# Last stage of a spectral mix and a decayed sum: channel-major result with gated last matrices, eight frequency units for nine, even places by accumulating transfers

## The chip, the cores and the metric

The kernel runs on one core of one Trainium2 chip. The core has a matrix engine (TensorE, PE in the profile, with PEld for its weight loads), a vector engine (DVE), a scalar engine (ACT), GpSimd (POOL), a queue engine that mostly issues transfers (SP), and 16 DMA engines. The engines share two memories: SBUF (128 partitions) and PSUM, which TensorE writes and DVE and ACT read. The metric is the device time of one execution in microseconds (us); lower is better.

## The reference

The input x has 2048 places and 512 channels. A gate g, one number for each place, mixes two results. The first is a filter in the frequency plane: a real two-dimensional Fourier transform, a product with complex weights, and the inverse. The second is a long convolution along the places with a kernel made from the channel's parameters, plus a skip term.

```python
g = sigmoid((x * gate_w).sum(-1, keepdims=True))
X = rfft2(x) * (w_r + 1j * w_i)
a = irfft2(X, s=(2048, 512))
dt = exp(log_dt)
A = -exp(log_A_real) + 1j * A_imag
C = (C_real + 1j * C_imag) * dt[:, None]
K = 2 * Re(einsum("dn,dnl->dl", C, exp(A * dt * pos)))
b = causal_conv(x, K) + x * D_skip
return g * a + (1 - g) * b
```

The arithmetic is float32. The kernel computes, per channel, whether `A * dt` is so small over 2048 places that K is a constant. If it is for all 512 channels (it is for these inputs), the convolution is a running sum of x times a number per channel, and the long general branch behind `tc.If` is not entered.

## The kernel before

**Order.** No scheduler is at work: `PLAN` is a list of words, a letter for a function and a number for its piece, and the program issues them in that order. Each engine works through its own words in that order. A tile of a pool (`ps` with 4 PSUM buffers, `blk` with `NBLK`, `w`, `v`, `short`) is reused once its last reader is done, so a word may also wait for a buffer.

**First stage** (`C`, `c`). x is loaded in pieces (`PARTS`). `C` runs small matrices over 64 partitions for each piece, for some pieces on sums and differences that POOL forms first (`F`); `c` turns the result on DVE (`STREAM_TRANSPOSE`) into `AR`. Every later unit reads all of `AR`.

**Middle stage, nine units.** The frequencies along the places are held in slots, two to a unit; unit 8 (`pr == 8`) is half as large and holds slot 0's and slot 16's leftovers. For each unit: `P` (TensorE, second transform), `t` (ACT copy to SBUF), `D` (TensorE, transform along channels), `d` (ACT copy), `Z` (four DVE instructions), `U` and `W` (DVE products with the weights), `p` and `g` (two POOL instructions each), `h` (ACT, one row), `I` (TensorE, transform back along channels), `i` (ACT copy) and `V` (two DVE instructions into `AI`). The weights of a unit are loaded by SP (`l`), and one row of them is overwritten (`L`).

**The running sum**, beside it, four quarters k of the channels. `x` and `y` (ACT) scale the even and the odd places; `m` is a DVE scan that gives the sums at the odd places; `n` (POOL) forms the even places by a subtraction; `o` (ACT) scales x by the skip factor; `r` (POOL queue) adds the sums to `XT` by a transfer of 1 MB that accumulates. `G` is the gate: TensorE, ACT, and a transfer that lays g with places on partitions (`g1`).

**Last stage.** `K` fixes slot 0, `B` (TensorE) and `b` (DVE transposes) give `VA`. The second result is brought from channels to places on partitions by TensorE transposes (`Y`), times 1 - g on the way out of PSUM (`s`, ACT). `Q` (TensorE) is the last matrix, eight blocks j of four matrices with 256 columns; `q` (DVE) or `a` and `A` (ACT, POOL) multiply by g and add, and SP stores.

Of the kernel before, what the change touches and what calls it, by code (L numbers as in the profile page):

```python
# [9 lines left out]
F32 = mybir.dt.float32  # L10
# [5 lines left out]
P = 128  # L16
# [4 lines left out]
NWARM = 10  # L21
NV = 2
# [16 lines left out]
PARTS = [slice(a, b) for a, b in zip([0, 4, 8, 16, 24, 32, 40, 48, 56], [4, 8, 16, 24, 32, 40, 48, 56, 64])]  # L39
# [3 lines left out]
def _consts():  # L43
# [37 lines left out]
    s2e = s2[:17][..., K2].reshape(17, 128, 128).transpose(1, 0, 2)  # L81
# [10 lines left out]
    s2p[2, 0, :, :, 1], s2p[2, 1, :, :, 1] = np.cos(th), -np.sin(th)  # L92

# [12 lines left out]
    s2r = np.stack([v.reshape(2, 32, 2, 128).transpose(2, 1, 0, 3).reshape(128, 128) @ inv for v in s2p[1:]], 1)  # L106
# [12 lines left out]
    s1b = s1b.reshape(32, 128, 64).transpose(1, 0, 2)  # L119
# [3 lines left out]
    for x in range(2):  # L123
# [29 lines left out]
        "c_s2v": f32(s2v), "c_s2r": f32(s2r), "c_s2q": f32(s2q), "c_s1b": f32(s1b), "c_s1a": f32(s1a.reshape(128, 4, 8, 128).transpose(1, 0, 2, 3)), "c_dfw": f32(dfw), "c_dbw": f32(dbw),  # L153
# [5 lines left out]
def body(ctx: ExitStack, tc: tile.TileContext, x, xg, xt, w, wh, prms, vecs, gw, dskip,  # L159
# [21 lines left out]
    AI = work.tile([P, 17, D], F32, name="AI")  # L181
# [28 lines left out]
    with tc.manual_schedule():  # L210
        prm = [blk([P, 4, P], "prm") for _ in range(3)]
        ldt = few[:, 0]
        nc.scalar.dma_start(s1e, c_s1e)
# [578 lines left out]
```

## Time and profile before

| | |
|---|---|
| time before, median of 3 runs | 131.91 us (130.80 to 132.53) |
| the profiled execution, its own time | 130.77 us |
| its span in the profile | 128.8 us |
| mean granted TensorE clock | 0.954 |
| ACT busy, share of the span | 61.9 us, 48% |
| DMA moved | 26.56 MB, mean 206 GB/s |

The span is shorter than the execution's own time by 1.97 us. In the rows of the timeline the first number is the start in us from the span's start, the second the time, `xN` the number of instructions in the row, and the bracket the idle time ahead of it with what ended it. Float32 matrices are recorded as two instructions each, so x16 is eight matrices.

### The profile page before, as it was taken

How to read it: one execution, taken by the hardware profiler on the slowest of the kernel's cores; microseconds unless marked ns; L12 is line 12 of the kernel's file. 1: busy time of each engine (PE TensorE's matmuls, PEld its weight loads, DVE VectorE, ACT ScalarE, POOL GpSimd, SP SyncE). 2: the span in 40 equal slices, each digit the busy share in tenths (PEclk: the TensorE clock that was granted, in tenths of full speed). 3: DMA queues.
4: the chain of work that ended last, by engine and by line, in shares of the span. 5: the costliest groups of instructions: out<-in, count | busy, mean ns of one | idle time of the engine just before them, and what ended most of it. 6: DMA issues, size and time to landing. Idle time of an engine off the chain costs nothing. (4 is left out here: it accounts for less than half of the span.)

```text
span 128.8 us, 2226 instructions
## 1 busy us (share of the span) xinstructions
PE 105.1 (82%) x817; PEld 84.5 (66%) x817; DVE 90.8 (70%) x136; ACT 61.9 (48%) x111; POOL 70.4 (55%) x62
## 2 busy tenths in 40 slices
PE   6988977699699999909949999398999999999000
PEld 6954646585189979809939599287844788898000
DVE  0077896897998889999975999982369935526500
ACT  0021007955339769997538354444760295464000
POOL 0467120427399999999959799993000000786000
PEclk9999999999999999996899999869999999999975
DMA  3999999999476299998288697250000003355960
GB/s 109 414 356 409 428 396 384 400 394 354 176 267 232 80 251 243 279 239 258 88 163 163 122 198 233 100 163 5 0 0 5 0 0 140 130 221 204 377 257 7
DMA packets 9300, 26.56 MB, mean 206 GB/s; under 512 B 1696, under 2 KB 2496, under 8 KB 8256
## 3 DMA queue, kind: packets, MB, share of 16 engines
q1 hardware_dynamic: 8560, 22.07, 46.0%
q0 software_dynamic: 576, 4.19, 16.9%
q8 instruction: 8, 0.13, 0.4%
q14 instruction: 12, 0.10, 0.2%
q10 hardware_dynamic: 144, 0.07, 0.2%
HBM read 17.90 MB, written 4.19 MB: 171 GB/s over the span
## 5 line engine op out<-in xcount | busy, mean ns | idle before, releaser
L376 PE MATMUL p_t<-s2e,AR 128*128 128x128 f32 x136 | 19.0, 299 | 3.1 <-DMA s2e<-in_c_s2e_dram 2.2
L376 PEld LDWEIGHTS p_t<-s2e,AR 128*128 128x128 f32 x136 | 18.1, 211 | 5.1 <-ACT gs L328 1.9
L458 PE MATMUL p_v<-dbw,gt 128*128 128x128 f32 x136 | 16.8, 278 | 4.2 <-DVE v L308 3.2
L458 PEld LDWEIGHTS p_v<-dbw,gt 128*128 128x128 f32 x136 | 15.9, 192 | 5.4 <-DVE v L308 3.4
L392 PE MATMUL p_d<-et,dfw 128*128 128x256 f32 (+1 forms) x72 | 16.6, 375 | 1.9 <-DVE v L308 1.7
L540 POOL TENSOR_TENSOR AI<-AI,qs 128x1024 f32<-128x1024 f32 x2 | 4.8, 2383 | 21.7 <-ACT qs L536 21.7
L263 DVE STREAM_TRANSPOSE AR<-p_s 128x512 f32<-128x512 f32 (+1 forms) x18 | 10.4, 629 | 7.6 <-PE p_s L255 6.9
L392 PEld LDWEIGHTS p_d<-et,dfw 128*128 128x128 f32 x72 | 12.6, 190 | 4.4 <-ACT XT L315 1.8
L312 POOL TENSOR_TENSOR v<-v,uo 128x1024 f32<-128x1024 f32 x4 | 10.1, 2536 | 8.7 <-DVE v L308 8.7
L525 PE MATMUL p_oa<-AR,s1a 128*128 128x256 f32 x64 | 14.3, 379 | 0.0
L471 DVE TENSOR_TENSOR AI<-p_v,po 128x512 f32<-128x512 f32 (+1 forms) x18 | 10.8, 649 | 5.0 <-ACT po L463 5.0
L427 POOL TENSOR_TENSOR px<-tw 128x512 f32<-128x512 f32 (+1 forms) x9 | 12.2, 1354 | 3.8 <-DVE tw L420 3.7
L525 PEld LDWEIGHTS p_oa<-AR,s1a 128*128 128x128 f32 x64 | 11.8, 187 | 1.9 <-DVE AR L493 0.2
L439 POOL TENSOR_TENSOR gt<-px 128x512 f32<-128x512 f32 (+1 forms) x9 | 12.5, 1384 | 0.3
L440 POOL TENSOR_TENSOR gt<-px 128x512 f32<-128x512 f32 (+1 forms) x9 | 12.4, 1381 | 0.0
L428 POOL TENSOR_TENSOR px<-tw 128x512 f32<-128x512 f32 (+1 forms) x9 | 12.2, 1353 | 0.0
L255 PE MATMUL p_s<-AI 64*64 64x256 f32 (+1 forms) x192 | 10.7, 363 | 1.8 <-issue 0.7
L501 PE MATMUL p_y<-eye,XT 128*128 128x128 f32 x64 | 10.0, 314 | 2.2 <-issue 2.2
L501 PEld LDWEIGHTS p_y<-eye,XT 128*128 128x128 f32 x64 | 9.2, 200 | 3.4 <-issue 2.3
L381 ACT COPY et<-p_t 128x1024 f32<-128x1024 f32 (+1 forms) x9 | 8.7, 961 | 5.2 <-PE p_t L376 5.2
L255 PEld LDWEIGHTS p_s<-AI 64*64 64x64 f32 x192 | 7.2, 132 | 5.6 <-PE p_s L250 2.4
L418 DVE TENSOR_TENSOR tw<-p_d,w 128x1024 f32<-128x1024 f32 x8 | 9.7, 1217 | 0.6 <-DVE p_d L405 0.5
(67 smaller groups left out, 165.9 us busy)
## 6 DMA issues: line engine op xcount, KB each, us to landing
XT<-in_xt_dram SPq DMA_DIRECT2D x4, 1024.0 KB
w<-in_w_dram SPq DMA_DIRECT2D x8, 512.0 KB, 5.2
XT<-v POOLq DMA_DIRECT2D x4, 1024.0 KB, 9.5
AI<-in_x_dram SPq DMA_DIRECT2D x7, 512.0 KB, 6.3
s1a<-in_c_s1a_dram SPq DMA_DIRECT2D x4, 512.0 KB, 4.0
out_dram<-bs SPq DMA_DIRECT2D x8, 256.0 KB, 2.3
out_dram<-AI SPq DMA_DIRECT2D x8, 256.0 KB, 3.6
prm<-in_prms_dram SPq DMA_DIRECT2D x3, 256.0 KB, 5.9
```

What stands on the lines that cost most here:

```text
L255: T.matmul(p[64 * g:64 * g + 64, h, u * n:u * n + n], s1e[r, 64 * u * i:64 * u * i + 64], xin(q)[r, i, g * n:g * n + n], start=i == 0, sto ...
L263: V.transpose(av[:, u, :, k], pv[:, u])
L376: T.matmul(p[:, q, :, 64 * v:64 * v + 64], AR[:, q % 2, 8 * (q // 2) + sl // 2, :, sl % 2], s2e[:, k], start=True, stop=True)
L392: T.matmul(parts(u)[:, o, 1:3] if h else parts(u)[:, o, 0:4:3], dfw[:, 2 * h + o], t_["et", u][:, 2 * h + o, :, :n], start=True, stop=True)
L427: G.tensor_tensor(po[:, 0], t1[:, :, 0:4:2], t1[:, :, 1:4:2][:, :, ::-1], op=ALU.subtract)
L428: G.tensor_tensor(po[:, 1, :, ::-1], t2[:, :, 0:4:2], t2[:, :, 1:4:2][:, :, ::-1], op=ALU.add)
L439: G.tensor_tensor(gv[:, :, 0], src[0], src[1], op=ALU.subtract)
L440: G.tensor_tensor(gv[:, ::-1, 1], src[0], src[1], op=ALU.add)
L458: T.matmul(p[:, v, h, o], rows(u, o, v, h), dbw[:, h, o], start=True, stop=True)
L471: V.tensor_tensor(ai[:, :, :, k], t_["pi", u][:, :n, :, 0], t_["po", u][:, :n], op=ALU.subtract if k else ALU.add)
L501: T.transpose(p[:, k, i], xv[:, i, :, 4 * j + k], eye)
L525: T.matmul(p[:, k], s1a[j // 2][:, 4 * j % 8 + k], VA[:, :, 4 * j + k], start=True, stop=True)
```

## The change

Four things are changed together, and the order is written anew.

1. **Eight units.** Slot 16's part is packed into the empty half of slot 0, so unit 8 is gone and every unit is full. Column 0 of unit 0 now needs a few tiny instructions of its own in `Z` and `h`; `K` has one matrix for two.
2. **Even places by a transfer.** The scan writes only the odd places' sums, into half the tile. `n` is now an accumulating transfer of 512 KB of `-x * scale` into the even half of `XT`, and `r` adds the sums to both halves from a source that is read twice. The places of `XT` are stored as two halves, even and odd.
3. **Channel-major result.** The last matrix takes `VA` as the stationary side and the constant `s1a` as the moving side, so the result has channels on partitions: eight blocks of eight matrices with 128 columns for eight blocks of four with 256. `Y`, `s` and the transposes of the second result are gone. g goes to DRAM and back as four broadcast tiles `gb` (`G2`, `O`). `E` (DVE) multiplies `s1a` by g, read from a copy in PSUM that `u` (ACT) makes; `H` (POOL) multiplies `XT` by 1 - g, 128 x 1024 at a time; `q` (DVE) is one addition for each block.
4. **First stage.** Ten pieces, nothing loaded between them, and POOL forms only the sum for eight of them (`FOLDS`), not the difference.

The general branch behind `tc.If` is adapted to the new layout; it is still not entered for these inputs.

```diff
-NWARM = 10
-NV = 2
+NWARM = 7
+NV = 4
-UNITS = [8, 0, 1, 2, 3, 4, 5, 6, 7]
+FOLDS = [0, 0, 1, 1, 1, 1, 1, 1, 1, 1]
-            E.tensor_tensor(f[:, 1, :n], xv[:, 0], xv[:, 1], op=ALU.subtract)
+            if FOLDS[q] == 2:
+                E.tensor_tensor(f[:, 1, :n], xv[:, 0], xv[:, 1], op=ALU.subtract)
...
-            v = t_["v", k] = work.tile([P, L], F32, tag="v", name="v", bufs=NV)
-            V.tensor_tensor_scan(v[:, 1:L:2], t_["v1", k], t_["uo", k], 0.0, op0=ALU.add, op1=ALU.add)
-
-        def even(k, E):
-            v = t_["v", k]
-            E.tensor_tensor(v[:, 0:L:2], v[:, 1:L:2], t_["uo", k], op=ALU.subtract)
+            t_["v", k] = work.tile([P, 1024], F32, tag="v", name="v", bufs=NV)
+            V.tensor_tensor_scan(t_["v", k], t_["ve", k], t_["vo", k], 0.0, op0=ALU.add, op1=ALU.subtract)
+
+        def even(k):
+            G.dma_start(part(2 * k), t_["vo", k], accum_op=ALU.add)
...
-            G.dma_start(XT[:, k], t_["v", k], accum_op=ALU.add)
+            G.dma_start(XT[:, k].rearrange("p (z n) -> p z n", z=2), t_["v", k].rearrange("p (o n) -> p o n", o=1).broadcast_to([P, 2, 1024]), accum_op=ALU.add)
+
+        def load_g(k):
+            t_["gb", k] = work.tile([P, 1024], F32, tag="v", name="gb", bufs=NV)
+            nc.sync.dma_start(t_["gb", k], gd[k // 2][1024 * (k % 2):1024 * (k % 2) + 1024].rearrange("(o n) -> o n", o=1).broadcast_to([P, 1024]))
+
+        def near(k):
+            t_["gp", k] = psum("p_g").rearrange("p u n -> p (u n)")
+            S.copy(t_["gp", k], t_["gb", 2 + k])
+
+        def damp(h, E):
+            r = part(h)
+            E.tensor_tensor(r, r, t_["gb", h % 2], op=ALU.mult)
...
+        def gated(k, E):
+            s = s1a[k].rearrange("p b (e c) -> p b e c", e=2)
+            g = (t_["gp", k // 2] if E is V else t_["gb", 2 + k // 2]).rearrange("p (b c) -> p b c", c=64)[:, 8 * (k % 2):8 * (k % 2) + 8]
+            for e in range(2):
+                E.tensor_tensor(s[:, :, e], s[:, :, e], g, op=ALU.mult)
+
         def Q_(j):
-            p = t_["pq", j] = psum("p_oa").rearrange("p k (b d) -> p (k b) d", b=2)
-            for k in range(4):
-                T.matmul(p[:, k], s1a[j // 2][:, 4 * j % 8 + k], VA[:, :, 4 * j + k], start=True, stop=True)
+            i, k = j // 4, j % 4
+            p = t_["pq", j] = psum("p_oa").rearrange("p u (b c) -> p (u b) c", b=4)
+            for b in range(8):
+                T.matmul(p[:, b], VA[:, i, 8 * (k % 2) + b, :, k // 2], s1a[k][:, b], start=True, stop=True)
+
+        def last_a(j, E, p):
+            i, k = j // 4, j % 4
+            o = AF_[:, 1024 * j:1024 * j + 1024]
+            z, b = k // 2, 8 * (k % 2)
+            xv = XT[:, 2 * i:2 * i + 2].rearrange("p e (z c b) -> p e z c b", z=2, b=16)[:, :, z, :, b:b + 8]
+            E.tensor_tensor(o.rearrange("p (e c b) -> p e c b", e=2, b=8), p.rearrange("p b (e c) -> p e c b", e=2), xv, op=ALU.add)
+            nc.sync.dma_start(out[j], o)
...
-        def q_a(j):
-            for k in range(4):
-                b = 4 * j + k
-                V.scalar_tensor_tensor(BS(j)[:, k], t_["pq", j][:, k], g1[:, 0, b:b + 1], BS(j)[:, k], op0=ALU.mult, op1=ALU.add)
-            store(j)
...
```

The order of SP from the last pieces of x on, before. `AI` is where x lands, `s2e` and `dfw` are the matrices of `P` and `D`, `w` is a unit's weights; the parameters `prm` stand ahead of these rows, among the pieces of x.

```order
L216 DMA AI_68<-in_x_dram 128x1024 x2
L296 DMA XT_69<-in_xt_dram 128x2048
L550 DMA s2e_71<-in_c_s2e_dram 128x256
L550 DMA s2e_71<-in_c_s2e_dram 128x128
L296 DMA XT_69<-in_xt_dram 128x2048
L556 DMA s2e_71<-in_c_s2e_dram 128x1024
L553 DMA eye_61<-in_c_eye_dram 128x128
L557 DMA gws_77<-in_gate_w_dram 128x128
L557 DMA pers_70<-in_vecs_dram 128x4
L552 DMA AI_68<-in_wh_dram 128x72
L551 DMA dfw_74<-in_c_dfw_dram 128x512
L362 DMA w_251<-in_w_dram 128x1024
```

And now:

```order
L229 DMA AI_71<-in_x_dram 128x512 x2
L282 DMA prm_109<-in_prms_dram 128x512
L282 DMA prm_111<-in_prms_dram 128x512
L554 DMA s2e_75<-in_c_s2e_dram 128x768
L279 DMA last_73<-in_vecs_dram 128x4
L282 DMA prm_257<-in_prms_dram 128x512
L555 DMA s2e_75<-in_c_s2e_dram 128x1024
L552 DMA eye_61<-in_c_eye_dram 128x128
L551 DMA last_73<-in_wh_dram 128x64
L392 DMA w_307<-in_w_dram 128x1024
L392 DMA w_316<-in_w_dram 128x1024
L550 DMA dfw_78<-in_c_dfw_dram 128x512
```

All of x goes ahead of the parameters, and the matrices of `P` and `D` and the first two units' weights go ahead of the 1 MB pieces of `XT`.

The end of POOL's order, before. `px` and `gt` are the results of `p` and `g` of the last two units, `qs` is a block scaled by ACT.

```order
L439 TENSOR_TENSOR gt_752<-px_729 128x2x4x64
L440 TENSOR_TENSOR gt_752<-px_729 128x2x4x64
L427 TENSOR_TENSOR px_765<-tw_761 128x2x2x128
L428 TENSOR_TENSOR px_765<-tw_757 128x2x2x128
L439 TENSOR_TENSOR gt_768<-px_765 128x2x4x64
L440 TENSOR_TENSOR gt_768<-px_765 128x2x4x64
L540 TENSOR_TENSOR AI_68<-AI_68,qs_968 128x1024
L540 TENSOR_TENSOR bs_826<-bs_826,qs_994 128x1024
L540 TENSOR_TENSOR AI_68<-AI_68,qs_1016 128x1024
```

And now, with the semaphores that a row waits for (`DMASW` those of POOL's own transfers, numbered in turn; `DMASW6` is that of the row `XT_72<-vo_710`). `vo` and `v` are the sources of `n` and `r`, `gb` holds 1 - g.

```order
L459 TENSOR_TENSOR gt_796<-px_788 128x2x4x64
L331 DMA XT_72<-vo_710 128x1024 [waits DMAHW0_49,Activation_49]
L349 TENSOR_TENSOR XT_72<-XT_72,gb_782 128x1024 [waits DMAHW7_49,DMASW4_49]
L349 TENSOR_TENSOR XT_72<-XT_72,gb_786 128x1024 [waits DMAHW0_49,DMASW5_49]
L337 DMA XT_72<-v_763 128x2x1024 [waits DMASW6_49,DVE_49,Activation_49]
L349 TENSOR_TENSOR XT_72<-XT_72,gb_782 128x1024
L349 TENSOR_TENSOR XT_72<-XT_72,gb_786 128x1024
L349 TENSOR_TENSOR XT_72<-XT_72,gb_782 128x1024 [waits DMASW2_49]
L349 TENSOR_TENSOR XT_72<-XT_72,gb_782 128x1024 [waits DMASW7_49]
L349 TENSOR_TENSOR XT_72<-XT_72,gb_786 128x1024 x2
```

Behind the last unit POOL had three additions of blocks; it has the last `n`, two products with 1 - g, the last `r` (which waits for that `n`) and six more products.

The end of DVE's order, before. `p_v` is a unit's last PSUM tile, `p_ia` and `p_oa` are the tiles of `B` and `Q`.

```order
L471 TENSOR_TENSOR AI_68<-p_v_802,po_811 128x2x2x128 x2
L471 TENSOR_TENSOR AI_68<-p_v_831,po_849 128x2x2x128 x2
L493 STREAM_TRANSPOSE AR_64<-p_ia_859 128x16x2x32
L493 STREAM_TRANSPOSE AR_64<-p_ia_865 128x16x2x32
L493 STREAM_TRANSPOSE AR_64<-p_ia_871 128x16x2x32
L493 STREAM_TRANSPOSE AR_64<-p_ia_881 128x16x2x32
L493 STREAM_TRANSPOSE AR_64<-p_ia_889 128x16x2x32
L493 STREAM_TRANSPOSE AR_64<-p_ia_894 128x16x2x32
L493 STREAM_TRANSPOSE AR_64<-p_ia_899 128x16x2x32
L493 STREAM_TRANSPOSE AR_64<-p_ia_906 128x16x2x32
L546 SCALAR_TENSOR_TENSOR bs_826<-p_oa_952,g1_62,bs_826 128x256 x4
L546 SCALAR_TENSOR_TENSOR AI_68<-p_oa_973,g1_62,AI_68 128x256 x4
```

And now, in two pieces: the last `V` with what stands among them (`s1a<-s1a,p_g` is `E`), and the last transposes.

```order
L528 TENSOR_TENSOR s1a_692<-s1a_692,p_g_694 128x8x64 x2
L528 TENSOR_TENSOR s1a_675<-s1a_675,p_g_694 128x8x64 x2
L328 SCALAR_TENSOR_TENSOR v_763<-p_x_744,vo_710 128x1024
L493 TENSOR_TENSOR AI_71<-p_v_724,po_746 128x2x2x128 x2
L493 TENSOR_TENSOR AI_71<-p_v_754,po_770 128x2x2x128 x2
L493 TENSOR_TENSOR AI_71<-p_v_772,po_799 128x2x2x128 x2
L373 CAST count_62<-p_count_791 1x1
L528 TENSOR_TENSOR s1a_702<-s1a_702,p_g_815 128x8x64 x2
L493 TENSOR_TENSOR AI_71<-p_v_806,po_819 128x2x2x128 x2
L528 TENSOR_TENSOR s1a_748<-s1a_748,p_g_815 128x8x64 x2
```

```order
L515 STREAM_TRANSPOSE AR_67<-p_ia_865 128x32x16x2
L515 STREAM_TRANSPOSE AR_67<-p_ia_870 128x32x16x2
L541 TENSOR_TENSOR AI_71<-p_oa_881,XT_72 128x1024
L515 STREAM_TRANSPOSE AR_67<-p_ia_875 128x32x16x2
L541 TENSOR_TENSOR AI_71<-p_oa_892,XT_72 128x1024
L541 TENSOR_TENSOR AI_71<-p_oa_904,XT_72 128x1024
L541 TENSOR_TENSOR AI_71<-p_oa_913,XT_72 128x1024
L541 TENSOR_TENSOR AI_71<-p_oa_935,XT_72 128x1024
```

Three of the four products with g and the last scan stand ahead of the last `V`, and the first addition of a finished block stands ahead of the last transpose; before, all eight transposes came first.

319 lines of the change are left out of this document (158 added, 161 removed).

## The prediction

> **What bounds the kernel now.** I read the busy time by stage first, then the timelines of DVE, POOL and TensorE, and last the transfers. The stages are cut at DVE's first `Z` (29.81), at the end of its last `V` (93.91) and at the end of its last addition (121.17).
>
> ```profile
> core 0: us, PE busy (x) PEld busy (x) DVE busy (x) ACT busy (x) POOL busy (x), PEclk, DMA share, GB/s
> 0.00:29.81 29.81, 24.86 (x289) 19.42 (x290) 19.01 (x30) 9.39 (x11) 10.70 (x17) 1.00 0.94 366
> 29.81:93.91 64.10, 54.80 (x371) 46.29 (x370) 54.32 (x78) 40.14 (x68) 52.59 (x43) 0.95 0.66 177
> 93.91:121.17 27.26, 25.45 (x158) 18.75 (x158) 17.46 (x28) 12.36 (x33) 7.10 (x3) 1.00 0.31 111
> 121.17:128.80 7.63, 0.00 (x0) 0.00 (x0) 0.00 (x0) 0.00 (x0) 0.00 (x0) 0.67 0.46 169
> ```
>
> The first stage is the transfers' (share 0.94), the last is TensorE's (25.45 of 27.26). In the middle three engines are near full. The DVE timeline tells which of them leads:
>
> ```profile
> 29.81 0.49 DVE L402 SCALAR_TENSOR_TENSOR p_d<-p_d,pers,ds 128x256 f32<-128x256 f32 x1 [0.73 <-ACT ds L396]
> 31.80 1.22 DVE L418 TENSOR_TENSOR tw<-p_d,w 128x1024 f32<-128x1024 f32 x1
> 34.07 0.48 DVE L402 SCALAR_TENSOR_TENSOR p_d<-p_d,pers,ds 128x256 f32<-128x256 f32 x1
> ...
> 51.28 1.27 DVE L471 TENSOR_TENSOR AI<-p_v,po 128x512 f32<-128x512 f32 x2
> 52.48 0.47 DVE L402 SCALAR_TENSOR_TENSOR p_d<-p_d,pers,ds 128x256 f32<-128x256 f32 x1
> ...
> 63.80 2.28 DVE L308 TENSOR_TENSOR_SCAN v<-p_x,uo 128x1024 f32<-128x1024 f32 x1
> 66.00 0.72 DVE L471 TENSOR_TENSOR AI<-p_v,po 128x256 f32<-128x256 f32 x2
> 68.85 0.49 DVE L402 SCALAR_TENSOR_TENSOR p_d<-p_d,pers,ds 128x256 f32<-128x256 f32 x1 [2.12 <-ACT ds L396]
> ...
> 89.27 1.29 DVE L471 TENSOR_TENSOR AI<-p_v,po 128x512 f32<-128x512 f32 x2 [2.89 <-ACT po L463]
> 92.62 1.29 DVE L471 TENSOR_TENSOR AI<-p_v,po 128x512 f32<-128x512 f32 x2 [2.06 <-ACT po L463]
> 95.16 9.17 DVE L493 STREAM_TRANSPOSE AR<-p_ia 128x1024 f32<-128x1024 f32 x8 [1.25 <-PE p_ia L490]
> ...
> 119.51 1.66 DVE L546 SCALAR_TENSOR_TENSOR AI<-p_oa,g,AI 128x256 f32<-128x256 f32 x4
> ```
>
> ```profile
> 34.30 1.26 POOL L427 TENSOR_TENSOR px<-tw 128x512 f32<-128x512 f32 x1 [2.73 <-DVE tw L420]
> ...
> 75.19 1.29 POOL L439 TENSOR_TENSOR gt<-px 128x512 f32<-128x512 f32 x1
> ...
> 80.25 1.27 POOL L439 TENSOR_TENSOR gt<-px 128x512 f32<-128x512 f32 x1
> ...
> 86.79 1.27 POOL L440 TENSOR_TENSOR gt<-px 128x512 f32<-128x512 f32 x1
> ...
> 115.60 2.38 POOL L540 TENSOR_TENSOR AI<-AI,qs 128x1024 f32<-128x1024 f32 x1
> ```
>
> From its first `p` at 34.30 POOL works until 88.06 almost without a break, and DVE's three long waits (2.12, 2.89, 2.06) are for results that come through it. So POOL paces the middle: `p` and `g` of a unit take 80.25 - 75.19 = 5.06.
>
> **The first stage.** Transfers and first units rest on these rows (page, then timelines):
>
> ```profile
> GB/s 109 414 356 409 428 396 384 400 394 354 176 267 232 80 251 243 279 239 258 88 163 163 122 198 233 100 163 5 0 0 5 0 0 140 130 221 204 377 257 7
> ```
>
> ```profile
> 10.88 1.27 POOL L240 TENSOR_TENSOR f<-AI 128x512 f32<-128x512 f32 x1 [0.92 <-DMA AI<-in_x_dram]
> ...
> 50.49 2.04 PE L376 MATMUL p_t<-s2e,AR 128*128 128x128 f32 x16
> ```
>
> ```profile
> 37.66 1.01 ACT L381 COPY et<-p_t 128x1024 f32<-128x1024 f32 x1 [2.54 <-PE p_t L376]
> ...
> 40.92 0.58 ACT L396 COPY ds<-p_d 128x512 f32<-128x512 f32 x1
> ```
>
> ```profile
> 38.72 1.99 PE L392 MATMUL p_d<-et,dfw 128*128 128x256 f32 x8 [0.21 <-ACT et L381]
> ```
>
> A slice is 3.22 us, so the bytes moved are 4.15 MB at 12.9, 5.53 at 16.1, 6.80 at 19.3 and 8.04 at 22.5; I keep that pace. The piece that POOL takes at 10.88 ends at 2.94 MB, moved by 9.9, so a piece lands about 1 us behind its bytes. Now x (4.25 MB with the first constants) lands at 14.1, and its last piece costs a POOL sum (0.7), matrices (0.6) and two DVE transposes (0.8): 16.2. The first `P` also needs `s2e`, which ends at 5.96 MB: 18.2. `D`'s matrix ends at 7.37 MB: 21.8. From 18.2 TensorE does `P` twice (2.04 each, and one transpose of 0.3 between), ending at 22.6, then `D` (1.99), ACT's `d` 0.58 and a hop of 0.1: first `Z` at 25.2, against 29.81. **-4.6.** Its bounds: 0 if the row of weights (`L`) or an order of landings holds it, -6 if `D` is not held by `P` of the second unit.
>
> POOL's saved differences, the warm-up's three matrices and the shorter parameter loads lie under the transfers here and count nothing.
>
> **The middle.** What goes: unit 8, four POOL subtractions of 2.4, the DVE step on `g1` (L333). What comes on DVE: `E`, on POOL four more transfers' issue. POOL would need 8 x 5.06 = 40.5 plus six issues, each nearest to
>
> ```profile
> L318 POOL DMA_DIRECT2D XT<-v x4 | 4.3, 1086 | 0.0
> ```
>
> so 47 from its first `p`. DVE needs, for each unit, `Z` 1.99 (31.80 - 29.81), `U` and `W` 2.27 (34.07 - 31.80) and `V` 1.20 (52.48 - 51.28): 8 x 5.46 = 43.7. Four scans at 2.20 (66.00 - 63.80): 8.8. Three pairs of `E` ahead of the last `V`, 128x512 with one input in PSUM like `V`: 3.6. The tiny pieces of unit 0: 0.4. Sum 56.5. So DVE leads now, and POOL trails its products by a unit. I add 3.0 for its waits, between the 8.4 it idled in this stage, of which POOL caused 7.1, and the 1.4 left without those. Stage 59.5 against 64.10: **-4.6**; the last `V` ends at 84.7. Bounds 57.9 and 64.9. The full cover of ACT (40.14 of 64.10 busy, less now) hides `u`'s two copies and the second sigmoid; if it is late, DVE's wait for `d` or `i` is what shows.
>
> **The transfers beside it.** Four `n` of 512 KB and four broadcasts of 512 KB are new.
>
> ```profile
> DMA to landing us min/median/max: 7.5/9.5/10.8
> ```
>
> ```profile
> q1 hardware_dynamic: 8560, 22.07, 46.0%
> q0 software_dynamic: 576, 4.19, 16.9%
> ```
>
> The first row is that of `r`, 1 MB. The accumulating queue used 16.9% of 128.8 = 21.8 for 4.19 MB, so 6.3 MB use 33; the other some 8 MB left after 32 us use 21 at q1's pace. That is 54 of the 60 us up to the last `r`: full, but not over. By bounds `n`, half as large, lands in 3.7 to 10.8; I take half of `r`'s, 5, as nearest. [...]
>
> **POOL's end.** The last unit's `g` ends at about 78.5 (DVE's last `U`, `W` near 72, then 5.06 and waits). Then the last `n` is issued; two `H` at 2.38 cover 4.8 of its landing; `r` is issued at about 84.5 and lands by 92 to 95.3; three more `H` end by then, and the last three end at 99.2 to 102.5. They are wanted from 104 on (below), so they cost nothing unless the transfers take 2 to 5 us more.
>
> **The last stage.**
>
> ```profile
> 92.79 8.43 PE L490 MATMUL p_ia<-AI,s2v 64*64 64x512 f32 x64
> 101.15 3.27 PE L501 MATMUL p_y<-eye,XT 128*128 128x128 f32 x24
> 104.38 10.68 PE L525 MATMUL p_oa<-AR,s1a 128*128 128x256 f32 x48
> ```
>
> Before, `Q` waited for all of `b` and for 24 transposes. Now the blocks j of one half of the channels need five transposes in DVE's order: the last `V` ends at 84.7, the first `b` starts 1.25 later, five take 5.7 (9.17/8 each): `Q` starts at 91.7. A block of `Q` is now eight matrices of 128 columns, like `P`'s eight: 2.04, against 1.78 (10.68/6) for four of 256. That is 2.1 more for the eight blocks, and it ends at 108.0; 64 `Y` of 128 columns are gone. The last addition follows: 128x1024 from PSUM, nearest to `W`'s 1.22, ends at 109.4, against 121.17. Stage 24.7 against 27.26: **-2.6.** Bounds: 22.6 at the old 1.78, and see the rival on the addition.
>
> The stores and the end are 7.63 as before: the last store is 512 KB for two of 256 KB.
>
> **Sum.** -4.6 - 4.6 - 2.6 = -11.8, from the execution's own 130.77: 119.0. That execution lies 0.9% under the median of 131.91, so the median of the changed kernel is 119.0 x 131.91/130.77 = 120.0.
>
> **The rivals.**
>
> - *The middle idles as before.* With DVE leading and POOL only one unit behind, a late `d` or `i` stops it at once. With 8.4 of waits for 3.0 the time is 5.4 more: 125.4. For it: PE, DVE and POOL all stay near full, and the DMA share rises. Against: the long waits named came through POOL, which loses 10 us of subtractions. If the early start is lost as well, 4.6 more: 130.0, no change.
> - *The last `r` ends the kernel.* If `n` and `r` both need 10.8, `r` is issued at 90 and lands at 101.5, and the last addition ends near 111: 121.6. It is faster all the same.
> - *The addition reads PSUM badly, and the kernel is slower.* `q` takes each element of `p_oa` 128 elements from the one before. No row reads PSUM so. DVE does three transposes and eight additions d after 91.7: the last ends at 95.1 + 8d. At d = 1.22 TensorE hides it; at 2.4 it ends at 114.3, the time 125; from d = 3.26 on it ends later than 121.17 and the gain is gone; at four times, 4.9, the time is 145. The rows speak for no penalty only in contiguous reads (`W` 1.22 for 1024, `V` 0.6 for 512). [...]
>
> **How the numbers follow.** About 2% is what a measurement of this kernel can tell from no change. The forecast as summed: 0.62, 116.5 to 122.5 by its own bounds. The middle idling: 0.18 at 125, and without the early start 0.05 at 130. The last `r`: 0.08 at 122. The additions at about twice: 0.04 at 125; slower than 3.3: 0.03. Faster by over 2% (under 129.3) are the first, second, fourth and fifth: 0.92; within 2%: 0.05; slower: 0.03. A range of 116 to 126 leaves out the cases at 130 and above, the ends of the others, and the unlikely good end.
>
> **What would show each step.** The first `Z` near 25; DVE with few waits from there to the last `V` near 85, where before it had three of over 2; a block of `Q` at 2.0 with no wait ahead of TensorE; additions of 1.2; POOL's last `H` ahead of the last `Q`. Wrong it would be made by an addition of over 2.4, by DVE waiting more than 8 between `Z` and `V`, or by a last addition that waits for POOL.

## The result, and the profile after

In the first comparison the changed kernel took 123.4 us (median of 4 runs, 121.18 to 124.47) and the kernel before 131.76 us (median of 4, 130.80 to 132.53): a ratio of 0.926, 95% interval 0.911 to 0.941. In a second one, beside the experiments, it took 122.19 us against 131.78, a ratio of 0.931 (0.923 to 0.939). It is faster, by 8.4 and 9.6 us in the medians, where 11.9 were forecast. The medians are over all executions, but the ratios and their intervals use only those within 1.5% of the fastest of the same kernel, so they are not the quotients of the medians, and a kernel with one such execution has no ratio.

The execution shown first took 124.47 us and has a lower granted TensorE clock than the others (0.892); a second one, at 0.943, took 120.55 us and is the one to be held against the profile before. Busy time by stage, cut at the first `Z`, the end of the last `V` and the end of the last addition, with the columns as before; first the execution at 0.892:

```profile
0.00:27.94 27.94, 22.73 (x315) 18.90 (x316) 13.05 (x31) 4.64 (x9) 10.50 (x18) 0.94 0.92 335
27.94:91.68 63.74, 50.72 (x320) 42.18 (x320) 55.85 (x79) 41.83 (x63) 49.51 (x40) 0.87 0.91 245
91.68:115.53 23.85, 22.58 (x192) 18.28 (x190) 19.88 (x19) 0.00 (x0) 17.66 (x8) 1.00 0.61 184
115.53:122.60 7.07, 0.00 (x0) 0.00 (x0) 0.00 (x0) 0.00 (x0) 0.00 (x0) 0.58 0.37 144
```

and the same kernel at 0.943:

```profile
0.00:27.86 27.86, 23.64 (x315) 19.89 (x316) 13.04 (x30) 4.64 (x9) 10.51 (x18) 0.94 0.89 326
27.86:88.15 60.29, 47.75 (x320) 40.08 (x320) 55.73 (x79) 41.72 (x63) 48.53 (x40) 0.94 0.93 257
88.15:112.27 24.12, 22.62 (x192) 18.67 (x190) 19.89 (x19) 0.00 (x0) 18.58 (x9) 1.00 0.65 198
```

Against before (29.81, 64.10, 27.26, 7.63) the second gains 1.95, 3.81, 3.14 and 1.10 us, 10.0 in all. The first gains 1.87, 0.36, 3.41 and 0.56. The two differ in the middle, 63.74 and 60.29, and DVE has the same work in both (55.85 and 55.73): the difference is waiting.

One place to look is TensorE's clock. The granted clock in 40 slices on the page, in tenths, of this kernel at 0.892 and at 0.943:

```profile
PEclk9999999599965799999999999955599999999955
```

```profile
PEclk9999998599997799999999999968999999999995
```

A slice is about 3 us. Three stretches are near half clock, around 21, 37 and 80 us. In TensorE's timeline (at 0.892) each comes behind a wait:

```profile
19.90 2.80 PE L402 MATMUL p_t<-s2e,AR 128*128 128x128 f32 x16 [2.54 <-DMA s2e<-in_c_s2e_dram]
22.49 0.42 PE L385 MATMUL p_h<-eye,last 128*32 128x128 f32 x1
22.70 2.85 PE L402 MATMUL p_t<-s2e,AR 128*128 128x128 f32 x16
...
36.78 3.75 PE L416 MATMUL p_d<-et,dfw 128*128 128x256 f32 x8 [4.02 <-DVE tw L443]
...
77.72 2.49 PE L483 MATMUL p_v<-dbw,gt 128*128 128x128 f32 x16 [3.03 <-DVE AI L493]
81.11 3.78 PE L483 MATMUL p_v<-dbw,gt 128*128 128x128 f32 x16 [0.91 <-ACT gt L465]
...
86.19 3.54 PE L483 MATMUL p_v<-dbw,gt 128*128 128x128 f32 x16 [1.03 <-ACT gt L465]
```

`P` takes 2.80 and 2.85 us for 2.05, `D6` 3.75 for 1.99, `I4` and `I5` 3.78 and 3.54 for 2.02.

The other place is POOL's queue, in its timeline of the same execution, then in that at 0.943:

```profile
40.51 1.28 POOL L459 TENSOR_TENSOR gt<-px 128x512 f32<-128x512 f32 x1
44.47 1.05 POOL L331 DMA_DIRECT2D XT<-vo  x1 [2.68 <-ACT XT L334]
48.53 0.86 POOL L331 DMA_DIRECT2D XT<-vo  x1 [3.00 <-ACT gt L464]
50.66 1.27 POOL L449 TENSOR_TENSOR px<-tw 128x512 f32<-128x512 f32 x1 [1.27 <-DVE AI L493]
```

```profile
43.74 1.05 POOL L331 DMA_DIRECT2D XT<-vo  x1 [2.00 <-ACT XT L334]
47.80 0.86 POOL L331 DMA_DIRECT2D XT<-vo  x1 [3.01 <-ACT gt L464]
48.91 1.27 POOL L449 TENSOR_TENSOR px<-tw 128x512 f32<-128x512 f32 x1 [0.25 <-issue]
```

Between `g2` and `p6` POOL does nothing but issue `n1` and `n2`, for which ACT must first have scaled `XT` (`o`): 8.9 us at 0.892, of which it is idle for 7. What `p6` itself waits for is not the `V` in the bracket, which is inferred: `p6` starts 0.1 to 0.2 us after the transfer of `n1` has landed (6.1 us after 44.47, and 5.0 after 43.74), and so it does in all nine profiles that issue `n1` there and have 13 block buffers. The landing took 5.0 to 8.2 us there. From `p6` on POOL works without a break to its last `g`. The last rows are groups of the page, DVE's additions, TensorE's last matrix and POOL's `H`:

```profile
L541 DVE TENSOR_TENSOR AI<-p_oa,XT 128x1024 f32<-128x1024 f32 x8 | 9.6, 1218 | 3.9 <-POOLq L574 2.6
L534 PE MATMUL p_oa<-s1a,AR 128*128 128x128 f32 x128 | 15.3, 282 | 0.0
L349 POOL TENSOR_TENSOR XT<-XT,gb 128x1024 f32<-128x1024 f32 x8 | 19.3, 2554 | 4.0 <-DMA gb<-gd 3.9
```

TensorE does its eight blocks in 15.3 us with no wait, and an addition takes 1.218 us.

### The profile page after: what moved, and what is told of

Its sections match the earlier page's. It is cut to its first block, busy times and chain, and to the rows that moved or that the text cites. A ratio compares the mean times of both kernels' runs of the same rounds, so it can differ in the third digit from the quotient of the medians.

```text
span 122.6 us, 2174 instructions
## 1 busy us (share of the span) xinstructions
PE 96.0 (78%) x825; PEld 79.4 (65%) x825; DVE 88.8 (72%) x126; ACT 46.5 (38%) x72; POOL 77.7 (63%) x66
## 4 chain that ended last, share of the span: by engine, by line
PE 39%; POOL 21%; DMA 12%; DVE 8%; issue 5%; ACT 4%; SPq 3%; DVEq 0%; POOLq 0%
PE p_oa L534 12%; DMA AI<-in_x_dram 8%; PE p_ia L511 6%; PE p_d L416 6%; PE p_v L483 6%; POOL px L449 6%; POOL gt L459 5%; POOL px L450 5%; DMA s2e<-in_c_s2e_dram 5%; PE p_t L402 4%; POOL gt L458 4%; PE p_gate L356 3%; SPq L229 3%; DVE tw L443 2%; DVE tw L441 2%
## 5 line engine op out<-in xcount | busy, mean ns | idle before, releaser
L349 POOL TENSOR_TENSOR XT<-XT,gb 128x1024 f32<-128x1024 f32 x8 | 19.3, 2554 | 4.0 <-DMA gb<-gd 3.9
L416 PE MATMUL p_d<-et,dfw 128*128 128x256 f32 x64 | 17.1, 419 | 6.1 <-DVE tw L443 4.0
L402 PEld LDWEIGHTS p_t<-s2e,AR 128*128 128x128 f32 x128 | 17.2, 212 | 2.9 <-issue 2.8
L449 POOL TENSOR_TENSOR px<-tw 128x512 f32<-128x512 f32 x8 | 11.9, 1485 | 7.8 <-DVE tw L443 6.5
L534 PEld LDWEIGHTS p_oa<-s1a,AR 128*128 128x128 f32 x128 | 15.2, 196 | 0.8 <-DVE AR L515 0.8
L534 PE MATMUL p_oa<-s1a,AR 128*128 128x128 f32 x128 | 15.3, 282 | 0.0
L493 DVE TENSOR_TENSOR AI<-p_v,po 128x512 f32<-128x512 f32 x16 | 10.2, 683 | 4.5 <-ACT po L487 4.5
L541 DVE TENSOR_TENSOR AI<-p_oa,XT 128x1024 f32<-128x1024 f32 x8 | 9.6, 1218 | 3.9 <-POOLq L574 2.6
L450 POOL TENSOR_TENSOR px<-tw 128x512 f32<-128x512 f32 x8 | 11.8, 1478 | 0.0
L458 POOL TENSOR_TENSOR gt<-px 128x512 f32<-128x512 f32 x8 | 10.7, 1332 | 0.5
L459 POOL TENSOR_TENSOR gt<-px 128x512 f32<-128x512 f32 x8 | 10.7, 1332 | 0.0
L264 PE MATMUL p_s<-AI,last 64*64 64x128 f32 (+1 forms) x192 | 9.5, 325 | 1.4 <-DMA AI<-in_x_dram 1.4
L441 DVE TENSOR_TENSOR tw<-p_d,w 128x1024 f32<-128x1024 f32 x8 | 9.8, 1221 | 0.3
L443 DVE TENSOR_TENSOR tw<-p_d,w 128x1024 f32<-128x1024 f32 x8 | 9.7, 1216 | 0.1
## 6 DMA issues: line engine op xcount, KB each, us to landing
XT<-v POOLq DMA_DIRECT2D x4, 1024.0 KB, 11.4
```

Of the source, the lines that this page charges most:

```text
L349: E.tensor_tensor(r, r, t_["gb", h % 2], op=ALU.mult)
L402: T.matmul(p[:, q, :, 64 * v:64 * v + 64], AR[:, q % 2, 8 * (q // 2) + u, :, v], s2e[:, 2 * u + v], start=True, stop=True)
L416: T.matmul(parts(u)[:, o, 1:3] if h else parts(u)[:, o, 0:4:3], dfw[:, 2 * h + o], t_["et", u][:, 2 * h + o], start=True, stop=True)
L441: E.tensor_tensor(t, z[:, :, ::-1], w, op=ALU.mult)
L443: E.tensor_tensor(t.rearrange("p o i k -> p (o i k)"), z.rearrange("p o i k -> p (o i k)"), w.rearrange("p o i k -> p (o i k)"), op=ALU.mult)
L449: G.tensor_tensor(po[:, 0], t1[:, :, 0:4:2], t1[:, :, 1:4:2][:, :, ::-1], op=ALU.subtract)
```

## The experiments

Two theories stood at the start, on why the middle took longer than forecast. *Queue*: POOL stands behind `n1` and `n2`, `p6` is late, and POOL then paces the middle. *Clock*: TensorE's half clock after its waits is what lengthens it. A third came up: DVE's own 56 us set the middle whatever else happens. The table gives the median of each run's comparison, and from its profile the first `Z` and the steps from there, in us.

| kernel | median (runs) | ratio, 95% | first Z | to p6 | to last g | to last V | to last addition |
|---|---|---|---|---|---|---|---|
| first profile | 123.4 (4) | 0.926 (0.911-0.941) | 27.94 | 22.72 | 34.99 | 6.03 | 23.85 |
| e1_base | 122.19 (4) | 0.931 (0.923-0.939) | 27.86 | 21.05 | 34.74 | 4.50 | 24.12 |
| e1_n_late | 128.80 (4) | none | 28.31 | 19.92 | 43.11 | 6.11 | 23.86 |
| e1_nblk14 | 123.14 (4) | none | 28.88 | 20.44 | 36.80 | 5.91 | 23.87 |
| e1_warm_p | 122.73 (6) | 0.924 (0.917-0.930) | 25.96 | 24.70 | 34.69 | 6.23 | 24.28 |
| e2_warm2 | 120.76 (6) | 0.918 (0.913-0.924) | 26.51 | 21.07 | 35.19 | 4.49 | 23.84 |
| e2_swapw | 121.81 (6) | 0.917 (0.912-0.923) | 26.75 | 22.82 | 34.95 | 5.69 | 23.89 |
| e2_n_pool | 123.65 (6) | 0.936 (0.929-0.942) | 28.51 | 22.04 | 36.24 | 4.50 | 23.85 |
| e2_e_sbuf | 134.62 (7) | 0.975 (0.967-0.983) | 26.81 | 22.68 | 36.76 | 5.97 | 34.21 |
| e3_no_e | 121.59 (6) | none | 28.60 | 21.44 | 35.12 | 6.28 | 24.19 |
| e3_no_nr | 118.42 (6) | 0.897 (0.893-0.902) | 26.28 | 17.80 | 36.03 | 5.60 | 23.89 |
| e3_warm3 | 123.33 (6) | 0.934 (0.929-0.939) | 26.95 | 20.92 | 35.37 | 6.37 | 23.87 |
| e3_h_dve | 120.36 (6) | 0.915 (0.910-0.920) | 26.51 | 21.10 | 35.44 | 4.49 | 23.84 |

**The changed kernel again** (e1_base).

> The changed kernel as it is, on the chip on which the other three of this set run, so that they have something to be set against. All theories: about 123.4 us, 0.926 of the kernel before; the first Z near 27.9 us, the last V near 91.7 us, the last addition near 115.5 us; POOL's waits of 2.7 and 3.0 us ahead of n1 and n2 and a wait of p6 to about 50.7 us are there again.

122.19 us; its profile is the second one above. The stages came as written but for the middle, which was 3.45 us shorter: `p6` started at 48.91, not 50.7, and the last `V` ended at 88.15.

**POOL's sums moved back** (e1_n_late).

```diff
-... g2 ... n1 o4 h2 ... n2 I2 ... p6 ... t4 g6 l5 h6 d1 r1 ... V6 U4 n3
+... g2 ... o4 h2 ... I2 ... p6 ... t4 g6 n1 n2 l5 h6 d1 ... V6 U4 r1 n3
```

> The issues of n1 and n2 move on POOL's queue behind g6, so that g3 to p6 no longer stand behind them, and r1 behind them. Theory of the queue (POOL loses 5.7 us in waits for outputs that ACT copies late, and 3.2 us more because p6 writes the buffer that n1's transfer reads, and paces the rest of the middle): p6 starts 3 to 6 us earlier, POOL's last g ends near 82 instead of 86.5 us, the last V near 88, and the kernel takes 119 to 121 us. Theory of the clock (TensorE's slow stretches after its gaps set the middle, and POOL's waits lie beside them): POOL's waits go elsewhere, the last V stays within 1 us of 91.7, and the kernel takes 122.5 to 124 us. If the moved sums make the ends of H late, 124 to 125.

128.8 us (125.44 to 129.65), 5.4 to 6.6 us over the medians of the kernel it was made from and slower than each of its executions. `p6` gained only 1.1 us after the first `Z` (19.92 for 21.05), since it now waited 6.05 us for a buffer that `I7` reads. The price was paid later, in DVE's timeline:

```profile
84.95 2.29 DVE L328 TENSOR_TENSOR_SCAN v<-p_x,vo 128x1024 f32<-128x1024 f32 x1 [5.22 <-DMA XT<-v]
```

The last scan waits 5.22 us for a `v` buffer that a late `r` still reads. The sums can't be moved back without that; the theory of the queue isn't settled by this run, only this cure is.

**One more block buffer** (e1_nblk14).

```diff
-NBLK = 13
+NBLK = 14
```

> One more buffer in the pool of large blocks (14 instead of 13), nothing else. Theory that the transfer of n1 holds the buffer that p6 wants: p6 starts at about 47.5 us, as soon as n2 is issued, instead of 50.7, POOL's work ends up to 3 us earlier, 120.5 to 122.5 us. Theory of the queue alone (the waits in front of n1 and n2 are what costs): these 5.7 us stay, and 123 to 124 us. Theory of the clock: 123 to 124 us.

123.14 us (119.88 to 124.75), no gain beside 122.19. `p6` started directly behind `n2`'s issue (49.32), 2.6 us before `n1`'s transfer landed, so its wait with 13 buffers is for the buffer that this transfer reads; but `g6` then waited 1.55 us for `p_v`, and the next step took 36.8 for 34.7.

**Eight dummy matrices ahead of `P7`** (e1_warm_p).

```diff
+            if u == 7:
+                for _ in range(8):
+                    T.matmul(p[:, 0, 0], ones, ones, start=True, stop=True)
```

> Eight matmuls of ones with ones (128 x 128, result overwritten by the first real matmul of the tile) stand in front of block P7, which begins as soon as its PSUM tile is free instead of when s2 has landed. Theory of the clock: TensorE isn't idle for 2.5 us ahead of P7, P7 and P2 take 2.0 to 2.2 instead of 2.80 and 2.85 us, the first Z comes 0.8 to 1.5 us earlier, and the kernel takes 121.5 to 122.7 us. Theory of the queue: the first Z comes earlier, but the middle waits for POOL all the same, and the kernel takes 123 to 124 us.

122.73 us. `P7` and `P2` took 2.12 and 2.05 us and the first `Z` came at 25.96, 1.9 earlier than 27.86. Of that, 0.42 is an earlier landing of `s2e` (`P7` at 19.46 for 19.88); the other 1.48 is the clock. From `P7` to the first `Z` it took 6.50 us for 7.98, and e2_e_sbuf, which has no dummies, bears it out: there `P7` took 2.12 us behind a wait of 2.16 us, and the step was 6.50 too, while in the five executions whose `P7` was slow it was 7.92 to 8.04. The second half of the other theory held too, in the execution shown: `p6` stood at 50.66 as in the first profile, with the half clock at 37 us still there (the gate took 4.75 us), and nothing was gained behind it.

**Both waits filled** (e2_warm2).

```diff
+        def again(u):
+            for _ in range(24):
+                T.matmul(t_["pt", u][:, 0, 0], ones, ones, start=True, stop=True)
-... P3 x2 ...
+... P3 Y6 x2 ...
```

> Eight dummy matmuls ahead of P7 as in the run before, and 24 more between P3 and D6, written over the PSUM tile of P6 once ACT has copied it (their result is read by nothing), so that TensorE's wait of 4.0 us there is filled; with them D6 gets another PSUM tile than U2's and need not wait for VectorE. Theory of the clock (the half clock after TensorE's waits is what lengthens P7 and P2, then D6 and the gate's matmuls, and these delay the scaled copies of ACT, the sums n1 and n2, p6 and all that POOL does after): granted clock 1.00 from 8 to 44 us, D6 2.0 and the gate 1.9 to 2.2 us, p6 at 45 to 47 us, last V 85 to 88 us, kernel 117.5 to 120.5 us, 0.90 to 0.92 of the kernel before. Theory that VectorE's own work sets the middle whatever the clock does: first Z near 26, then the same 60.3 us to the last V, 86.3 us, kernel 119.5 to 120.5 us with p6 at 48 us or later. Theory of POOL's queue: p6 stays at 48.5 to 50.7 us, last V 88 to 91.5 us, 122 to 123.4 us.

The eight ahead of `P7` are in it too. 120.76 us, the lowest span so far, 118.1. TensorE's timeline from `P7` on, and its clock in 40 slices:

```profile
19.88 2.12 PE L405 MATMUL p_t<-s2e,AR 128*128 128x128 f32 x16 [0.40 <-DMA s2e<-in_c_s2e_dram]
...
31.18 5.52 PE L409 MATMUL p_t<-last 128*128 128x128 f32 x48
36.54 1.89 PE L423 MATMUL p_d<-et,dfw 128*128 128x256 f32 x8
38.36 3.64 PE L356 MATMUL p_gate<-XT,gws 128*32 128x512 f32 x32
```

```profile
PEclk9999999999999999999999999769999999999965
```

Two of the three stretches are gone, the one near 76 us remains; `D6` takes 1.89 us. The gate takes 3.64 at full clock, so I was wrong to expect 2.0 to 2.2. `p6` is at first `Z` + 21.07 as without dummies at 0.943, and 1.65 sooner than in the execution at 0.892: `n1` was issued 15.33 us after the first `Z` for 15.88 at 0.943, but its transfer took 5.6 us for 5.0. The last `V` ended 60.75 us after the first `Z`, for 60.29, so in this profile the dummies shortened the first stage and not the middle. `p6` at 47.58 and the median lie between the bands, and the run doesn't choose among the theories. Six runs spread from 119.91 to 122.06. The interval of the ratio just meets that of the second comparison, so a gain of about 1% is likely, not shown beyond it.

**One dummy for 24** (e2_swapw).

> The same with a single dummy matmul between P3 and D6 in place of 24: D6 needs no longer wait for U2's PSUM tile and starts near 31 us, and TensorE waits ahead of the gate (for the loads of the last input slabs, near 36 us) in place of ahead of D6. Theory of the clock: the wait is about 2 to 4 us, and the gate runs at half clock if it is over 2.3 us (3.6 us instead of 2.0); D3 all the same starts 1.5 to 4 us earlier than at 43.8 us, since D6 no longer stands between; kernel 118.5 to 121 us, slower than with 24 dummies by 0 to 2 us. Theory of the PSUM tile (only the wait for it matters, not the clock): the same time as with 24 dummies, within 0.7 us.

The edit is the one above with `range(1)`. 121.81 us, a ratio that can't be told from the one with 24. `D6` started at 31.87 and `D3` at 39.28, 2.65 earlier than with 24, and `n1` was issued at 41.26, 0.8 us earlier after the first `Z` than with 24. Yet `p6` came at first `Z` + 22.82, for the transfer of `n1` took 8.2 us for 5.6. TensorE next waited 2.73 us for the load of `dbw`, and its next block took 3.12 us. Removing the wait for PSUM alone moves the wait.

**Even places by POOL again** (e2_n_pool; undoes part 2 of the change as far as `n` goes).

```diff
-            G.dma_start(part(2 * k), t_["vo", k], accum_op=ALU.add)
+            G.tensor_tensor(part(2 * k), part(2 * k), t_["vo", k], op=ALU.add)
```

> The four even places of the running sum by POOL additions again (128 x 1024 each, in the same places of the order) in place of accumulating transfers. POOL gets 4 x 2.4 us and loses 4 x 0.6 to 0.9 us of issuing, three of them ahead of the last V; p6 no longer waits for n1's landing (0.2 to 3 us). Theory that POOL paces the middle from p6 on: last V 2.5 to 5 us later, kernel 124.5 to 127 us. Theory that VectorE or the clock paces it and POOL has room: within 1 us of the changed kernel, 121.5 to 123.5 us.

123.65 us, between the bands of the two theories. The cost is 0.5% by the ratios, inside their intervals. POOL's step from `p6` to the last `g` grew by 1.5 us, one `n` of 2.4 less its issue; the two ahead of `p6` fell mostly into time in which POOL waited anyway. The last `V` came 62.78 us after the first `Z` for 60.29, which is the 2.5 us of the theory that POOL paces the middle. What accumulating transfers for these four sums bought is about 0.6 us by the ratios, not shown to differ from nothing.

**`E` from SBUF** (e2_e_sbuf; the copies `u` do nothing any more).

```diff
-            g = (t_["gp", k // 2] if E is V else t_["gb", 2 + k // 2])...
+            g = t_["gb", 2 + k // 2]...
```

> The products E read the gate from SBUF in place of ACT's copy in PSUM, and the copies u are gone, so that two PSUM tiles less are wanted between 70 and 92 us. Theory that the copies take the PSUM tiles which I4 and I5 wait for, and that TensorE's half clock there follows from that wait: TensorE waits under 2 us ahead of I4, granted clock 1.00 from 76 to 88 us, last V 1 to 3.5 us earlier, kernel 119.5 to 121.5 us. Rival: the wait ahead of I4 is for V0 or V1, which VectorE reaches no sooner, and E reads slower beside POOL (0.62 us becomes up to 1.2 us, 8 of them): last V the same or later, kernel 122 to 126 us.

134.62 us in the median: three executions took 127.43 to 128.89, four 134.62 to 143.25, and these lie above the kernel before. The rival came, and worse than written. The products on DVE, by line, then POOL's `H` beside them and TensorE's wait:

```profile
L528 DVE TENSOR_TENSOR s1a<-s1a,gb x8: 670/1753/8187, 75.7 to 94.9; 128x512 f32<-128x512 f32 x8
```

```profile
95.16 14.92 POOL L349 TENSOR_TENSOR XT<-XT,gb 128x1024 f32<-128x1024 f32 x6
```

```profile
104.31 5.59 PE L511 MATMUL p_ia<-AI,s2v 64*64 64x512 f32 x32 [8.24 <-DVE AR L515]
```

The numbers are the least, median and longest in ns: 0.67 us alone, 8.19 us for the one that began at 94.9, as POOL's row of `H` started. TensorE then waited 8.24 us for DVE, and the last stage took 34.21 us. Without the copies `u` into PSUM most of the gain is gone: the ratio is 0.975 for 0.931.

**DVE relieved** (e3_no_e; here and below the edit is to e2_warm2's kernel).

```diff
-... S1 u0 h0 ... S2 E1 E0 I1 ... u1 E3 i5 ... r0 E2 H7 ...
+... S1 h0 ... S2 I1 ... i5 ... r0 H7 ...
```

> The kernel with both groups of dummies (118.1 us span in the profile, last g of POOL 82.8, last V 87.3 us), without the products E and the copies u: the last matrices stay ungated, so the output lacks the gate in its last part. VectorE loses 8 x 0.68 us, 4.1 of them (E0, E1, E3) ahead of the last V. Theory that VectorE's work sets the middle: last V near 83.2 us, kernel 4 us faster than with E, 116 to 117.5 us. Theory that POOL sets its end (last V = last g + 4.5 us in every fast execution): last g stays within 1 us of 82.8, last V within 1 us of 87.3, VectorE waits 4 us more for copies of ACT, and the kernel takes 119 to 121 us. If the PSUM tiles that u frees let I4 start earlier: granted clock 1.00 near 80 us in both cases.

The step from the first `Z` to the last `g` was 56.56 us (56.26 with `E`), so 3.6 us less work on DVE in the middle (52.16 for 55.75) moved nothing; DVE waited instead, in its timeline of the last two `V`:

```profile
84.34 1.29 DVE L500 TENSOR_TENSOR AI<-p_v,po 128x512 f32<-128x512 f32 x2 [1.97 <-ACT po L494]
...
90.15 1.29 DVE L500 TENSOR_TENSOR AI<-p_v,po 128x512 f32<-128x512 f32 x2 [4.47 <-ACT po L494]
```

121.59 us, some 0.6 above the band for POOL's theory, with a late first `Z` (28.60: TensorE waited 1.38 us for `dfw`) and a half clock near 85 us in the execution shown. The theory of DVE, 116 to 117.5, falls.

**POOL relieved** (e3_no_nr).

```diff
-... n1 o4 ... n2 ... d1 r1 ... U4 n3 r2 ... p1 r3 ... B5 n0 H5 H6 r0 ...
+... o4 ... d1 ... U4 ... p1 ... B5 H5 H6 ...
```

> The kernel with both groups of dummies, without the eight accumulating transfers n and r: the running sum isn't added to the skip term, so the output lacks it. POOL loses their issues (0.6 to 1.2 us each, three n and three r ahead of the last V), the waits of 1.5 and 3.0 us ahead of n1 and n2, and the wait of p6 for n1's landing; 6.3 MB of transfers go too. Theory that POOL sets the end of the middle: p6 at 43 to 45 us, last g 74 to 78, last V 80 to 82.5 us, kernel 112.5 to 115.5 us. Theory that VectorE's 57 us of work set it: last V at first Z + 58 to 59.5 us, 84.5 to 86.5 us, kernel 117.5 to 119.5 us, however early POOL is done.

118.42 us, ratio 0.897. Now POOL waits for DVE's products, in its timeline:

```profile
44.08 1.28 POOL L456 TENSOR_TENSOR px<-tw 128x512 f32<-128x512 f32 x1 [3.90 <-DVE tw L450]
...
59.84 1.27 POOL L456 TENSOR_TENSOR px<-tw 128x512 f32<-128x512 f32 x1 [5.59 <-DVE tw L450]
```

The last `V` ends 59.43 us after the first `Z`. That is DVE's theory in this kernel (58 to 59.5); POOL's (80 to 82.5 us for the last `V`) falls, since it ends at 85.71. With e3_no_e it gives both bounds: DVE with its own waits allows about 59.4 us for the middle, POOL with its queue about 60.3 to 60.8 (e1_base, e2_warm2). They lie some 1.1 us apart, which is why relieving DVE gained nothing in the middle and relieving POOL only 1.3 us. The 6.3 MB of accumulating transfers went too, so what the transfers themselves cost isn't separated.

**A third group of dummies** (e3_warm3).

```diff
+        def refill(k):
+            for _ in range(10):
+                T.matmul(t_["ve", k][:, 0:P], ones, ones, start=True, stop=True)
-... I1 m0 V0 ...
+... I1 m0 w0 V0 ...
```

> The kernel with both groups of dummies and a third: ten matmuls over the PSUM tile of x0 after the scan has read it, ahead of I4, which gets another PSUM tile by this and no longer waits for V0. Theory of the clock: TensorE's wait of 3.0 us ahead of I4 falls under 2, granted clock 1.00 to 88 us, I4 and I5 2.0 us each in nearly every execution (3.8 and 3.5 us in the slower ones before), median 119 to 120.3 us, and a narrower spread than 119.9 to 122.1. Theory that POOL's last g sets the last V: the fast executions stay at 119.9 us, only the slow ones gain, median 119.9 to 120.8 us.

123.33 us: slower than with two groups (0.934 against 0.918). My reading of the trace was wrong: the wait of 3.0 us stands ahead of `I1`, not `I4`. In TensorE's timeline:

```profile
75.54 3.43 PE L494 MATMUL p_v<-dbw,gt 128*128 128x128 f32 x16 [3.04 <-DVE AI L504]
80.03 2.50 PE L324 MATMUL p_x<-last 128*128 128x128 f32 x20 [1.06 <-DVE v L332]
82.37 1.95 PE L494 MATMUL p_v<-dbw,gt 128*128 128x128 f32 x16
```

The dummies wait for the scan, and `I4` behind them starts at 82.37, where it had followed `I1` at once. So the run tells the price of a late `I4` (last `g` to last `V` 6.37 us for 4.49), and nothing on the clock there.

**Two `H` on DVE** (e3_h_dve).

```diff
-... Q3 Q2 q5 H2 H0 q2 ...
+... Q3 Q2 q5 M2 M0 q2 ...
```

> The kernel with both groups of dummies, with the last two damping products H2 and H0 on VectorE in place of POOL. Theory that TensorE (B 7.75 and Q 15.3 us without waits) sets the last stage and POOL's H has room: the last addition ends where it did or 0 to 2.5 us later (VectorE gets 2 x 1.2 to 2.4 us and has waits of 3.4 us there), kernel 120.5 to 123 us. Theory that POOL's last H is waited for: the end comes 0.5 to 2.5 us earlier, 118 to 120.2 us.

120.36 us, the same as without the edit. POOL's last `H` ended at 102.79 for 107.14, and the last stage took 23.84 us in both.

## Why the prediction was right, and where it was not

The forecast of 120.0 lies 3.4 and 2.2 us under the medians measured; the direction and the range held. At 0.943 the stages gained 10.0 of the 11.8 us: 2.65 and 0.79 us were missing in the first two, and 0.54 and 1.10 us more than forecast in the last two hide part of that, which is luck for the sum. No run undid parts 1, 3 or 4 of the change, so how they share the gain isn't shown.

- **First stage, -4.6: measured -1.95.** Two steps failed. "I keep that pace": the transfers moved 326 to 335 GB/s over this stage where they had moved 366. The 5.96 MB up to the end of `s2e` were moved by about 18.1 us, not 17.2 (an estimate from the page's GB/s by slices, as in the prediction), `s2e` landed 1.8 us behind them, not 1, and the first `P` started at 19.88, not 18.2. Why the pace fell wasn't tried. And "TensorE does `P` twice (2.04 each)": with the transpose they took 5.6 us for 4.4, at half clock after a wait that the prediction itself had made (TensorE idle until `s2e` lands). That part is shown: with the dummies they took 4.1 us (19.88 to 23.99 in e2_warm2), and the first `Z` came at 25.96 to 26.95 in six kernels; only in e3_no_e, with its wait for `dfw`, at 28.60. Without dummies it came at 27.86 to 28.88, but for the 26.81 of e2_e_sbuf, whose clock had not fallen.
- **Middle, -4.6: measured -3.81, and -0.36 at the lower clock.** DVE's work was sized well (56.5 against 55.7 busy). By the brackets, as the prediction counts them, it waited 3.2 us at 0.943 and 6.5 at 0.892, where 3.0 were forecast. The step that failed is "DVE leads now, and POOL trails its products by a unit", with 47 us for POOL from its first `p` to its last `g`: it took 52.4 and 54.3, because I had counted `n`'s issues as work of POOL, and not what its queue waits for ahead of them, nor the landing of `n1` that `p6` waits for. Less work on DVE moved nothing (e3_no_e), and the last `V` ended 4.5 us behind POOL's last `g`. That the stage still came within 0.8 us of 59.5 is luck: the bounds by DVE and by POOL lie about 1 us apart. Without `n` and `r` it took 59.43 us. The 7.1 us that the prediction puts down to POOL in the kernel before were also read wrongly in part: ahead of DVE's wait of 2.12 us `D` had waited for DVE's own scan, in TensorE's timeline before:

```profile
66.23 1.97 PE L392 MATMUL p_d<-et,dfw 128*128 128x256 f32 x8 [1.67 <-DVE v L308]
```

- **The remaining difference of 3.45 us between the two executions** is 1.67 ahead of `p6`, 0.25 up to the last `g` and 1.53 behind it. The prediction had no term for the clock, though the row of the middle before showed 0.95. Of the first part 0.65 is what `D6` and the gate took longer at the lower clock (3.75 and 4.16 us for 3.62 and 3.64), by which `n1` was issued later; the other 1.0 is that its transfer landed in 6.1 us for 5.0, whose cause is open. The last part is the clock by the durations: in seven profiles `I5`, the last unit's `I`, took 3.23 to 3.78 us for 2.05, and the step from the last `g` to the last `V` was longer than 4.50 by that difference within 0.1 us. No run held the clock up there.
- **Transfers.** The channels' share in the middle was 0.93, against 54 of 60 us. `n` landed in 6.6 us (median), for 5 within 3.7 to 10.8; `r` took 11.4, over its bound of 10.8. From the view of transfers:

```profile
XT<-v POOLq DMA_DIRECT2D x4, 1024.0 KB, 11.4
XT<-vo POOLq DMA_DIRECT2D x4, 512.0 KB, 6.6
```

- **POOL's end, last `H` at 99.2 to 102.5: measured 109.89** at 0.943, with `r0` issued at 93.24 for 84.5: the last `g` came 5.2 us later than forecast, and the two `H` ahead of `r0` waited 4.1 us for `gb`, for which there was no term. Part of the condition of the rival of the last `r` came true, its price did not: the additions waited 0.5 us for POOL at 0.943, but `Q` itself ended only at 110.77 there, and taking two `H` from POOL changed nothing. The 2.6 us put down to POOL's queue on the page of the first profile recur at the same place as a wait for TensorE in e1_base and e2_warm2.
- **Last stage, -2.6: measured -3.14.** A block of `Q` took 1.92 us (15.34/8) for 2.04. The additions took 1.218 us, so the rival of the strided read is out.
- **The end, 7.63 as before: measured 6.53 and 7.07.** I had taken no gain there.
- **The middle idling, 0.18 at 125.4**, is what the execution at 0.892 came nearer to: DVE waited 6.5 of the 8.4 us named, by another way than named.

Of the kernels that give the whole result, those with both groups of dummies (0.918), with one dummy for 24 (0.917) and with two `H` moved besides (0.915) have the lowest ratios; they can't be told from each other, and they are about 1% under the changed kernel (0.931), with intervals that just meet or just part.

## What to carry to other kernels

A word that only issues a transfer still holds its queue until its input is ready (`n1` and `n2` held POOL's for 2.7 and 3.0 us in the first profile): add to an engine's work the waits ahead of each issue, and name what stands behind it, and who writes the buffer that the transfer reads. Before relieving an engine, find the second bound by a run that relieves another one; here they lay about 1 us apart. Where a change opens a wait of over 2 us in TensorE, price the matrices behind it once at full and once at half clock: here both came (`P7` 2.12 us behind a wait of 2.16, 3.61 behind 2.34).

## What the runs showed of the hardware

- TensorE's granted clock fell to about half (0.50) after waits of 2.3 to 4.0 us and stayed there for some 3 to 10 us, but not after every such wait: the blocks behind 2.75 us (e3_no_e), 3.01 (e1_warm_p) and 3.04 (e2_e_sbuf) took 2.0 us as at full clock. Behind the same wait of 3.0 us it was back by 82 us at 0.943 and by 90 at 0.892. Ahead of `P7` a wait of 2.34 us was enough in e1_base (3.61 us), while one of 2.16 in e2_e_sbuf was not (2.12 us). What decides between the two is not shown.
- A DVE product with both inputs in SBUF took up to 8.19 us for 0.67 beside POOL's products (e2_e_sbuf), and 0.68 to 0.69 us with one input in PSUM (e1_base). The longest took longer than one `H` beside it (2.4 us).
- Dummy matrices put into TensorE's waits did not make the next block later than without them (e1_base): `P7` started at 19.46 us (e1_warm_p) and 19.88 (e2_warm2) for 19.88, `D6` at 36.54 (e2_warm2) for 36.71. The kernel took 2.6 us longer where they themselves waited for an engine (e3_warm3).
- The same accumulating transfer of 512 KB, `n1`, landed in 5.0 to 8.2 us, in nine profiles with other traffic beside it (DMA share 0.91 to 0.94 over the middle in three of them).
